# Decay factors by TensorE from sums of logarithms, and the float64 weights converted inside the attention

## The chip, the cores and the metric

The kernel runs on one core of one Trainium2 chip. The metric is the device time of one launch in microseconds (us). Five engines work side by side: TensorE (PE in the rows, with its weight loads as PEld), VectorE (DVE), ScalarE (ACT), GpSimd (POOL), and SyncE (SP), which here issues most DMAs. Each engine runs its own instructions in the order in which the program issued them; a semaphore holds an instruction, and all behind it on that engine, until what it needs is there.

## The reference

Three stages follow each other: a gated linear attention, an expert layer with a greedy routing of fixed capacity, and a feed-forward layer with ELU. The weights of the last stage, `w_in` and `w_out`, are float64.

```python
f = 1.0 / (1.0 + np.exp(-f_logit))                    # 4 batches, 8 heads, 768 steps, 48 channels
for t in range(S):
    state = f[:, :, t, :, None] * state + np.einsum('bhd,bhe->bhde', k[:, :, t], v[:, :, t])
    y[:, :, t] = np.einsum('bhd,bhde->bhe', q[:, :, t], state)
...
logits = x @ w_gate                                   # x: 3072 tokens of 384; 8 experts, 384 tokens each
for idx in np.argsort(-logits.flatten()):             # a token takes an expert that is not yet full
    ...
out[mask] = np.maximum(x[mask] @ w1[e], 0.0) @ w2[e]  # 384 -> 1024 -> 384, per expert
...
h = x @ w_in                                          # 384 -> 2048
return np.where(h > 0, h, np.exp(np.minimum(h, 0)) - 1) @ w_out
```

## The kernel before

**Attention** (lines 343 to 678). The 3072 tokens are 24 chunks of 128, six to a batch. Inside a chunk the recurrence is written with the running product W of 1/f: keys are multiplied by W, queries divided by it, and the chunk is then two small matrix products and a carried state. The layout has channels on partitions (two heads of 48 in slots of 64) and time along the row. The steps of a chunk, by name:

- `prepE` (line 420): ACT makes vv = 1 + exp(-f_logit) in two passes. `prepA` (line 428): DVE runs a scan over the 512 elements of a row, W, with a restart value `rst` at the head of each 128, and takes the last reciprocal into `pend`.
- `prepB`: ACT makes P = 1/W as exp(-ln W). `prepK`, `prepC` (lines 443 to 455): POOL makes kk = k W, aa = q P and W P; `prepD`: DVE makes qq = (2 - W P) aa, which takes out the error of the logarithm.
- `scores` (line 465): PE multiplies kk by qq, head by head; `masked`: DVE masks the result into `am`; `turn`: PE transposes kk, ACT copies it to `kn`.
- `ystep` (line 494): PE adds am v and S qq into y; PE makes kv, DVE puts it into the state SA (lines 518, 519), and `carry` copies the state on ACT to S, which the next chunk's matmul on line 507 reads.
- `xrows` (line 530): PE turns y to rows and multiplies it by `wg` (lp), ACT copies the rows, SP writes them to DRAM; `best` and `count` prepare the routing.

**Float64 words.** [...] The class `Conv` (line 258) takes a block of words as pairs of 32-bit integers and makes two float32r parts of them: `load` (a DMA into r64), `bits` (three DVE operations, lines 299, 303, 306, the middle one for the block before), `hi` (ACT, line 312) and `lo` (POOL, line 319). A block has 256 columns; there are 48. The tables ATT_CONV, SURE_CONV, GAP_CONV, F_CONV, M_AHEAD and M_CONV say how many are handled at which place: the 24 of `w_in` in the attention, the 24 of `w_out` after it, in the routing, in the first expert and in the first group.

**Routing and feed-forward.** After the attention a grid of thresholds finds the tokens whose expert is certain (lines 679 to 819; a branch for other inputs is not taken). Then PE works through eight experts, each with F1 (line 1056) and F2 (lines 1043 to 1045), and after each expert through a group of the last layer: A (line 1183, `w_in`) and B (`w_out`). Expert 0 goes first with 256 of its tokens, so that its 16 blocks of matmuls and its group cover the rest of the routing: rounds of `rows`, four `compare`s on DVE (lines 881 to 884), `ranks` on PE (line 891), `assign`, `left`, `again`, then `pick`. These stand between the matmuls at fixed places: a call of `tick` after each block of matmuls issues what is due. The experts' own weights are split into two parts by `feed` (ACT line 234, POOL line 227).

```python
blocks = wi_blocks + wo_blocks                     # line 251
r = self.pool.tile([128, 256, 2], I32, name="r64", bufs=4)
...
for _ in range(F_CONV[f]):                         # line 1141, in the first expert
    conv_stage()                                   # lo, hi, bits, load
```

Of the kernel before, what the change touches and what calls it, by code (L numbers as in the profile page):

```python
# [23 lines left out]
ATT_RAW = (11, 12)                          # chunks that load weights of the experts ahead  # L24
# [3 lines left out]
M_AHEAD = (0, 1, 1, 1)  # L28
M_CONV = (1, 2, 0, 2, 1, 2, 1, 0, 0, 2, 3, 3, 0, 0, 1, 2)
# [141 lines left out]
def kernel(ctx, tc, fT, kT, qT, v, wg, w12, win, w_out, out):  # L171
# [11 lines left out]
    win_h = wts.tile([128, 3 * 2048], F32R, name="win_h")  # L183
    win_l = wts.tile([128, 3 * 2048], F32R, name="win_l")
    WO1 = 6 * 384    # columns of w_out that are split early
    wout = [[wts.tile([128, WO1], F32R, name=f"wout{p}") for p in "hl"]]
# [3 lines left out]
    # the other experts run in the order in which they fill; None is the next of them  # L190
# [7 lines left out]
    # halves of the pieces, in the order of their use: w1 of f + 2, then w2 of f  # L198
# [8 lines left out]
    def raw():  # L207
        """Loads the next half, if its expert is known."""
# [12 lines left out]
    def feed(n, eng=None):  # L221
        """Splits up to n halves into their two parts; the low part of one goes with the high part of the next."""
# [15 lines left out]
    used = [-1, -1]     # the last piece whose w1, w2 were used before the current block  # L238
# [10 lines left out]
    wi_blocks = [("i", c, k) for k in range(8) for c in range(3)]  # L249
    wo_blocks = [("o", i) for i in range(24)]  # L250
    blocks = wi_blocks + wo_blocks

    def wo_cols(c, n):
        """Both parts of n columns of w_out."""
        k = c >= WO1
        return [t[:, c - k * WO1:c - k * WO1 + n] for t in wout[k]]
# [113 lines left out]
    load(0, "v")  # L370
    load(2, "f")
    load(1, "kq")
    load(2, "kq")
    load(1, "v")
    load(2, "v")
    for t in VT:
# [922 lines left out]
```

## Time and profile before

| what | us |
|---|---|
| three timed runs | 907.32, 914.92, 913.14 (median 913.14) |
| span of the profiled execution, first to last instruction | 910.4 |
| PE busy in it | 821.4 (90%) |
| DVE, ACT, POOL busy | 547.8, 443.5, 347.9 |
| mean granted TensorE clock, share of full speed | 0.935 |

The profile tells of one execution; its span is the only time that it gives of that one, and it lies 2.7 us under the median of the timed runs. An engine's busy time is the union of its instructions; waiting is not busy. The granted clock is given as a share: 1.00 is the upper level of 2.4 GHz, 0.5 the lower of 1.2 GHz, and a value between is a mean over time at both. In the attention DVE is busy nearly all the time, in the rest PE is.

### The profile page before, as it was taken

What the parts mean: (1) busy time and instruction counts of PE and PEld (TensorE: products, weight loads), DVE (VectorE), ACT (ScalarE), POOL (GpSimd) and SP (SyncE); (2) the same over time, 40 slices, a digit from 0 to 9 for tenths busy, and PEclk for the clock granted to TensorE, in tenths of its full rate; (3) what the DMA queues carried; (4) which work ended last, traced back from release to release, by engine and by line L of the source; (5) the groups of instructions that cost most, each with busy time, mean ns of one, the idle gap of its engine ahead of it and who ended that gap; (6) DMA issues with size and microseconds to landing.
All of it is one profiled execution on the core that took longest, in us unless ns stands there. A gap on an engine that the chain in (4) does not pass through costs nothing.

```text
span 910.4 us, 15321 instructions
## 1 busy us (share of the span) xinstructions
PE 821.4 (90%) x5573; PEld 776.8 (85%) x5573; DVE 547.8 (60%) x1245; ACT 443.5 (49%) x954; POOL 347.9 (38%) x379
## 2 busy tenths in 40 slices
PE   5977777895877799999999999999999999999996
PEld 4766666683867698999999999899999999999996
DVE  8799999987789867656756434533332432432332
ACT  5755555552344435444443544554444544544443
POOL 5667667844644654008103501351026107204101
PEclk7898897888777899999999999999999999999999
DMA  6556556433323332005101300630015004201000
GB/s 209 180 187 199 165 197 216 144 115 123 97 65 98 114 95 72 17 1 152 41 1 61 100 15 22 198 120 18 1 36 147 18 1 129 63 1 62 1 1 27
DMA packets 52037, 79.87 MB, mean 88 GB/s; under 512 B 9584, under 2 KB 34416, under 8 KB 51952
## 3 DMA queue, kind: packets, MB, share of 16 engines
q1 hardware_dynamic: 48752, 69.34, 24.6%
q0 software_dynamic: 3200, 9.46, 3.2%
q8 instruction: 46, 0.75, 0.3%
q14 instruction: 39, 0.32, 0.1%
HBM read 69.24 MB, written 9.54 MB: 87 GB/s over the span
## 4 chain that ended last, share of the span: by engine, by line
PE 54%; issue 9%; DVE 9%; POOL 2%; ACT 1%; POOLq 0%; DVEq 0%
PE ha L1183 18%; PE ha L1056 9%; PE yo L1043 9%; PE yo L1045 8%; PE yo L1044 8%; DVE oh L884 1%; DVE oh L881 1%; POOL pc_l L227 1%; PE ha L1038 1%; DVE w L306 1%; DVE w L299 1%; DVE w L303 1%; DVE oh L883 1%; DVE h_l L1061 1%; DVE elu L1187 0%
## 5 line engine op out<-in xcount | busy, mean ns | idle before, releaser
L227 POOL TENSOR_TENSOR pc_l<-raw,pc_h 128x384 fp32r<-128x384 f32 x128 | 131.4, 1049 | 84.6 <-ACT pc_h L234 57.2
L1187 DVE SCALAR_TENSOR_TENSOR elu<-elu,ha 128x384 f32<-128x384 f32 (+2 forms) x128 | 70.8, 553 | 151.6 <-ACT elu L1186 151.0
L1254 POOL DMA_INDIRECT out<-ot,permL x22 | 22.5, 1023 | 291.7 <-ACT ot L1252 288.4
L1183 PE MATMUL ha<-yt_h,win_h 128*128 128x384 f32 (+2 forms) x384 | 132.3, 345 | 0.5 <-DVE elu L1187 0.5
L1183 PE MATMUL ha<-yt_h,win_l 128*128 128x384 f32 (+2 forms) x384 | 130.9, 341 | 0.0
L1043 PE MATMUL yo<-wouth,g_h 128*128 128x384 f32 x381 | 130.5, 343 | 0.0
L1045 PE MATMUL yo<-wouth,g_l 128*128 128x384 f32 x381 | 129.5, 340 | 0.0
L1044 PE MATMUL yo<-woutl,g_h 128*128 128x384 f32 x381 | 129.0, 339 | 0.0
L1183 PE MATMUL ha<-yt_l,win_h 128*128 128x384 f32 (+2 forms) x384 | 127.0, 338 | 0.0
L1185 ACT ACTIVATE elu<-ha 128x384 f32<-128x384 f32 (+2 forms) x128 | 62.6, 489 | 114.6 <-PE ha L1183 114.5
L1025 ACT ACTIVATE g_h<-elu 128x384 fp32r<-128x384 f32 (+2 forms) x127 | 66.5, 523 | 75.9 <-DVE elu L1187 75.6
L1026 DVE TENSOR_TENSOR g_l<-elu,g_h 128x384 fp32r<-128x384 f32 (+2 forms) x112 | 66.1, 591 | 55.5 <-ACT g_h L1025 54.9
L1061 DVE SCALAR_TENSOR_TENSOR h_l<-ha,h_h 128x384 fp32r<-128x384 f32 (+2 forms) x72 | 36.8, 511 | 91.2 <-ACT h_h L1060 85.7
L1060 ACT ACTIVATE h_h<-ha 128x384 fp32r<-128x384 f32 (+2 forms) x72 | 32.6, 453 | 107.4 <-PE ha L1056 96.4
L1183 PEld LDWEIGHTS ha<-yt_h,win_h 128*128 128x128 f32 x384 | 73.9, 192 | 2.2 <-DVE elu L1187 0.7
L1183 PEld LDWEIGHTS ha<-yt_h,win_l 128*128 128x128 f32 x384 | 73.5, 191 | 2.2
L1183 PEld LDWEIGHTS ha<-yt_l,win_h 128*128 128x128 f32 x384 | 73.0, 191 | 1.4
L1043 PEld LDWEIGHTS yo<-wouth,g_h 128*128 128x128 f32 x381 | 72.4, 190 | 0.9 <-ACT g_h L1025 0.3
L1044 PEld LDWEIGHTS yo<-woutl,g_h 128*128 128x128 f32 x381 | 72.4, 190 | 0.6
L1056 PE MATMUL ha<-xt_h,pc_h 128*128 128x384 f32 (+2 forms) x216 | 71.3, 331 | 1.7 <-ACT pc_h L234 0.8
L1045 PEld LDWEIGHTS yo<-wouth,g_l 128*128 128x128 f32 x381 | 72.3, 190 | 0.3 <-DVE g_l L1026 0.3
L1056 PE MATMUL ha<-xt_h,pc_l 128*128 128x384 f32 (+2 forms) x216 | 71.2, 330 | 0.7 <-POOL pc_l L227 0.7
(248 smaller groups left out, 1831.5 us busy)
## 6 DMA issues: line engine op xcount, KB each, us to landing
raw<-w SPq DMA_DIRECT2D x144, 192.0 KB, 2.6
ld_k<-kT SPq DMA_DIRECT2D x24, 256.0 KB, 3.3
ld_q<-qT SPq DMA_DIRECT2D x24, 256.0 KB, 4.0
r<-win SPq DMA_DIRECT2D x24, 256.0 KB, 4.5
r<-wout SPq DMA_DIRECT2D x24, 256.0 KB, 2.7
ld_f<-fT SPq DMA_DIRECT2D x23, 256.0 KB, 4.1
vt<-v SPq DMA_DIRECT2D x24, 192.0 KB, 4.0
x_d<-x SPq DMA_DIRECT2D x24, 192.0 KB, 2.1
```

The costliest lines, as they stand in the source:

```text
L227: (eng or nc.gpsimd).tensor_tensor(l, RAW.pop(i), h.bitcast(F32), op=OP.subtract)
L1025: nc.scalar.activation(hi, src, AF.Copy)
L1026: (eng or nc.vector).tensor_tensor(lo, src, hi.bitcast(F32), op=OP.subtract)
L1043: nc.tensor.matmul(o, wh, mh, start=start, stop=False)
L1044: nc.tensor.matmul(o, wh, ml, start=False, stop=False)
L1045: nc.tensor.matmul(o, wl, mh, start=False, stop=stop)
L1056: nc.tensor.matmul(p[:, :n], a[:, d * 128:(d + 1) * 128], b[:, d, :n], start=i == 0, stop=i == 8)
L1060: nc.scalar.activation(h[:, :n], p[:, :n], AF.Relu)
L1061: nc.vector.scalar_tensor_tensor(l[:, :n], p[:, :n], 0.0, h[:, :n].bitcast(F32), op0=OP.max, op1=OP.subtract)
L1183: nc.tensor.matmul(p, a[:, d * 2048 + f * 128:d * 2048 + (f + 1) * 128], b[:, d, :N], start=i == 0, stop=i == 8)
L1185: nc.scalar.activation(e, p, AF.Relu, scale=-1.0)
L1187: nc.vector.scalar_tensor_tensor(e, e, -1.0, p, op0=OP.add, op1=OP.max)
```

## The change

The decay factors come from a sum of logarithms. `f_logit` is loaded a second way, token by token (`fN`); ACT makes u = ln(1 + exp(-f_logit)) in two passes (`decayE`, `decayL`), and PE multiplies u by the triangular mask, which sums it over time (`decays`, eight products into one PSUM tile L, channels on partitions). ACT makes W = exp(L), P = exp(-L) and `pend` from L. POOL makes kk, DVE qq = q P; the scan, the correction of P and two of POOL's three products are gone. The state is kept in the layout in which PE reads it, so ACT's copy of it is gone; the product with it has eight matmuls for four. The loop over the chunks issues each result one step ahead of its use. Scores have one buffer of two PSUM banks instead of three of one; W, P, u, x have fewer SBUF buffers.

The blocks of float64 words have 512 columns, there are 24, one per chunk, all of them in the attention; the tables for the later places are gone, and with them every conversion after the attention. `r64` has 2 buffers of 4 KB per partition instead of 4 of 2 KB. Both weights lie whole in SBUF from the start.

In the routing the comparison with the threshold uses a value `least` that ACT computes from tau, and a few checks of ranges are added.

```diff
-ATT_CONV = [0] * 4 + [2, 2, 1, 2, 1, 1, 2, 1, 1, 2, 1, 1, 2, 1, 1, 1, 2] + [0] * 3
-SURE_CONV, GAP_CONV, GAP_LOADS = 2, 5, 4
-F_CONV = (1, 1, 2, 1, 0, 1, 1, 0)
+ATT_CONV = range(0, 24)
-            r = self.pool.tile([128, 256, 2], I32, name="r64", bufs=4)
+            r = self.pool.tile([128, CW, 2], I32, name="r64", bufs=2)
-                w = self.pool.tile([128, 256], I32, name="w64", bufs=4)
+                w = self.pool.tile([128, CW], I32, name="w64", bufs=3)
-        nc.vector.tensor_tensor_scan(fl(W), fl(vv), fl(rst[:, h]), 1.0, op0=OP.mult, op1=OP.min)
+    L = ps.tile([112, 4, 128], F32, name="L")
...
+    def decayE(j):
+        if j < NJ:
+            nc.scalar.activation(buf(j, "u", [128, 384], 3), T[j]["f"], AF.Exp, scale=-1.0, accum_out=usum[:, j:j + 1])
+    def decayL(j):
+            nc.scalar.activation(u, u, AF.Ln, bias=1.0)
+    def decays(j):
+        for pr in range(4):
+            for s in range(2):
+                o = (2 * pr + s) * 48
+                nc.tensor.matmul(L[s * 64:s * 64 + 48, pr, :], u[:, o:o + 48], mask, start=True, stop=True)
+    def prepW(j):
+            nc.scalar.activation(buf(j, "W", HD, 1), L, AF.Exp)
+    def prepP(j):
+            nc.scalar.activation(buf(j, "P", HD, 1), L, AF.Exp, scale=-1.0)
+            nc.scalar.activation(pend[:, j], L[:, :, 127], AF.Exp, scale=-1.0)
...
-            SK[j] = [ps.tile([128, 4, 128], F32, name="sc", bufs=3) for s in range(2)]
+        SK[j] = ps.tile([128, 2, 4, 128], F32, name="sc")
...
-                nc.tensor.matmul(y[0:112, pr, :], Sc[:, pr].rearrange("p s e -> p (s e)")[:, :112],
-                                 c["qq"][0:112, pr], start=False, stop=True, skip_group_check=True)
+                for s in range(2):
+                    r = slice(s * 64, s * 64 + 48)
+                    nc.tensor.matmul(y[r, pr, :], S[j % 2][r, pr], C[j]["qq"][r, pr], start=False, stop=True,
+                                     skip_group_check=True)
...
-    for j in range(3, NJ):
+    for j in range(-5, NJ):
+            load(j + 7, "f")
+            load(j + 3, "kq")
+            load(j + 2, "v")
             conv.load()
+            prepW(j + 2); prepP(j + 2); prepK(j + 2)
+            state(j)
+            scores(j + 1); turn(j + 1)
+            xout(j - 2)
+            decayL(j + 4)
+        decayE(j + 5)
+            carry(j)
+            prepQ(j + 2)
+            lout(j - 2)
+        conv.lo()
+        conv.hi()
+        conv.bits()
+            turned(j + 1); masked(j + 1)
+            ystep(j); yout(j)
+            xrows(j - 1)
+            decays(j + 3)
...
-                    for _ in range(F_CONV[f]):
-                        conv_stage()
-            for _ in range(M_AHEAD[f] if si == NE else 0):
-                conv_stage()
```

The first place is VectorE in one chunk in the middle of the attention, of before, with one conversion block (w and r are the words of a block, SA the state, am the masked scores):

```order
L299 TENSOR_SCALAR w_1081<-r_1000 128x256
L303 SCALAR_TENSOR_TENSOR w_989<-r_901,w_989 128x256
L306 SCALAR_TENSOR_TENSOR w_1081<-r_1000,w_1081 128x256
L460 SCALAR_TENSOR_TENSOR qq<-P,aa 128x512
L491 TENSOR_TENSOR am_1124<-sc,mask 128x512
L491 TENSOR_TENSOR am_1125<-sc,mask 128x512
L432 TENSOR_SCALAR rst<-vv 128x4
L433 SCALAR_TENSOR_TENSOR W<-vv,rst 128x512
L434 RECIPROCAL pend<-W 128x4
L518 TENSOR_TENSOR SA<-kv,SA 112x192
L519 TENSOR_TENSOR SA<-SA,pend 112x192
L542 TENSOR_REDUCE Lall<-lp 128x8
```

The row of line 433 is the scan. The same engine in a chunk of the change:

```order
L497 TENSOR_TENSOR SA<-kv,S_149 112x192
L498 TENSOR_TENSOR S_148<-SA,pend 112x192
L445 TENSOR_TENSOR qq<-ld_q,P 112x512
L535 TENSOR_REDUCE Lall<-lp 128x8
L286 TENSOR_SCALAR w_1128<-r_1083 128x512
L290 SCALAR_TENSOR_TENSOR w_1033<-r_988,w_1033 128x512
L293 SCALAR_TENSOR_TENSOR w_1128<-r_1083,w_1128 128x512
L478 TENSOR_TENSOR am<-sc,mask 128x1024
```

The scan, its restart value and the reciprocal are gone, the conversion has blocks twice as wide, and the state stands at the head of the chunk, before the conversion. Line 286 reads the block r that this chunk loads, line 290 the block of the chunk before.

The second place is SyncE's queue of DMAs in one chunk of the attention, of before (ld_k, ld_q, ld_f, vt are the inputs, r the words of a block, x_d the rows of x):

```order
L363 DMA ld_k<-kT 128x512
L363 DMA ld_q<-qT 128x512
L360 DMA vt_105<-v 128x384
L363 DMA ld_f<-fT 128x512
L289 DMA r_1373<-win 128x512
L540 DMA x_d<-x 128x384
```

And of the change:

```order
L352 DMA ld_f<-fN 128x384
L355 DMA ld_k<-kT 112x512
L355 DMA ld_q<-qT 112x512
L349 DMA vt_103<-v 128x384
L276 DMA r_1175<-wout 128x1024
L532 DMA x_d<-x 128x384
```

The block of words has twice the bytes and still stands behind the four inputs; the inputs are a little smaller.

The third place is VectorE in the first round of the routing, inside expert 0, of before (oh and mr belong to the `compare`s, h_l to F1):

```order
L881 TENSOR_SCALAR oh<-mr,m_4414 128x128
L883 TENSOR_SCALAR oh<-mr,m_4414 128x384
L884 SCALAR_TENSOR_TENSOR oh<-mr,m_4414,triS 128x128
L299 TENSOR_SCALAR w_4702<-r_4560 128x256
L303 SCALAR_TENSOR_TENSOR w_4652<-r_4475,w_4652 128x256
L306 SCALAR_TENSOR_TENSOR w_4702<-r_4560,w_4702 128x256
L1061 SCALAR_TENSOR_TENSOR h_l<-ha,h_h 128x256
L881 TENSOR_SCALAR oh<-mr,m_4414 128x256
```

And of the change:

```order
L843 TENSOR_SCALAR oh<-mr,m_4396 128x128
L845 TENSOR_SCALAR oh<-mr,m_4396 128x384
L846 SCALAR_TENSOR_TENSOR oh<-mr,m_4396,triS 128x128
L1023 SCALAR_TENSOR_TENSOR h_l<-ha,h_h 128x256
L843 TENSOR_SCALAR oh<-mr,m_4396 128x256
```

The conversion between one comparison and the next is gone; the rest stands as it did.

## Rows read from the trace of the kernel before

**Rows 1.** Busy time of each engine in stretches of the span, with granted clock.

```profile
core 0: us, PE busy (x) PEld busy (x) DVE busy (x) ACT busy (x) POOL busy (x), PEclk, DMA share, GB/s
0.00:18.00 18.00, 9.02 (x61) 6.96 (x63) 15.39 (x33) 9.76 (x18) 9.38 (x23) 0.78 0.72 248
45.00:203.00 158.00, 126.81 (x1263) 107.14 (x1261) 152.53 (x313) 87.98 (x202) 107.25 (x83) 0.86 0.55 175
203.90:227.40 23.50, 12.84 (x130) 9.73 (x129) 16.54 (x48) 5.60 (x15) 9.60 (x23) 0.88 0.40 123
227.40:258.10 30.70, 25.51 (x172) 24.15 (x173) 25.09 (x63) 10.28 (x27) 18.25 (x21) 0.72 0.32 95
258.10:319.10 61.00, 44.65 (x313) 42.82 (x312) 52.14 (x140) 28.73 (x75) 34.02 (x43) 0.82 0.32 93
319.10:354.00 34.90, 32.44 (x201) 31.40 (x201) 25.26 (x51) 13.46 (x30) 18.06 (x19) 0.95 0.35 103
408.30:436.20 27.90, 26.81 (x193) 25.86 (x192) 19.81 (x43) 11.99 (x27) 19.76 (x22) 1.00 0.46 135
```

**Rows 2.** Timeline of TensorE at single places: start, duration, what (us).

```profile
3.55 4.12 PE L569 MATMUL sc<-triU,onesB 128*128 128x256 bf16 x22 [3.55 <-DVE onesB L386]
...
15.98 2.08 PE L503 MATMUL y<-am,vt 128*64 128x128 f32 x15 [3.36 <-DVE am L491]
...
199.71 1.10 PE L503 MATMUL y<-am,vt 128*64 128x128 f32 x16
200.73 1.13 PE L507 MATMUL y<-qq,S 112*112 112x128 f32 x8
201.70 1.05 PE L534 MATMUL lp<-IW,yt 112*128 112x120 f32 x8
```

**Rows 3.** Single lines of VectorE over the whole span: duration ns min/median/max.

```profile
L433 DVE TENSOR_TENSOR_SCAN W<-vv,rst x25: 692/1226/2334, 4.8 to 178.9; 128x512 f32<-128x512 f32 x23, 128x256 f32<-128x256 f32 x2
L306 DVE SCALAR_TENSOR_TENSOR w<-r,w x48: 409/418/1493, 55.7 to 302.2; 128x256 int32<-128x256 int32 x48
L299 DVE TENSOR_SCALAR w<-r x48: 278/289/1255, 55.4 to 301.6; 128x256 int32<-128x256 int32 x48
L460 DVE SCALAR_TENSOR_TENSOR qq<-P,aa x24: 426/680/1755, 8.6 to 192.7; 128x512 f32<-128x512 f32 x22, 128x256 f32<-128x256 f32 x2
L491 DVE TENSOR_TENSOR am<-sc,mask x56: 398/677/686, 15.5 to 198.5; 128x512 f32<-128x512 f32 x40, 128x256 f32<-128x256 f32 x16
L519 DVE TENSOR_TENSOR SA<-SA,pend x16: 357/766/1245, 28.6 to 199.5; 112x192 f32<-112x192 f32 x16
```

**Rows 4.** Groups of POOL in 45 to 203 us: busy us, mean ns.

```profile
L446 POOL TENSOR_TENSOR kk<-ld_k,W 128x512 f32<-128x512 f32 x17 | 23.9, 1409 | 18.7 <-DMA ld_k<-kT 10.4 <-DVE w L306 4.9 <-DVE qq L460 1.7
L319 POOL TENSOR_TENSOR win_l<-w,win_h 128x256 fp32r<-128x256 f32 x24 | 20.3, 851 | 5.5 <-ACT win_h L312 5.5
```

**Rows 5.** DMA issues in 30 to 200 us: size, median us from issue to landing.

```profile
r<-win SPq DMA_DIRECT2D x24, 256.0 KB, 4.5
```

**Rows 6.** What TensorE waited for in 227 to 350 us: total, times, longest.

```profile
PE rt L891 <- DVE oh L881: 14.6, 8, 3.9
PE rt L948 <- DVE oc L942: 4.1, 2, 3.5
```

**Rows 7.** Groups of VectorE and POOL in 227.4 to 319.1 us: busy us, mean ns.

```profile
L306 DVE SCALAR_TENSOR_TENSOR w<-r,w 128x256 int32<-128x256 int32 x20 | 12.0, 598 | 0.0
L303 DVE SCALAR_TENSOR_TENSOR w<-r,w 128x256 int32<-128x256 int32 x20 | 11.0, 552 | 0.0
L299 DVE TENSOR_SCALAR w<-r 128x256 int32<-128x256 int32 x20 | 8.1, 404 | 0.0
...
L319 POOL TENSOR_TENSOR woutl<-w,wouth 128x256 fp32r<-128x256 f32 x21 | 16.5, 791 | 3.4 <-ACT wouth L312 3.4
```

**Rows 8.** Timeline of TensorE inside expert 0: two matmuls that follow each other.

```profile
238.76 0.28 PE L1056 MATMUL ha<-xt_h,pc_h 128*128 128x256 f32 x1
238.88 0.28 PE L1056 MATMUL ha<-xt_l,pc_h 128*128 128x256 f32 x1
```

More of the change, by code (lines that the diff above doesn't have):

```diff
@@ L170, with kernel @@
 @with_exitstack
-def kernel(ctx, tc, fT, kT, qT, v, wg, w12, win, w_out, out):
+def kernel(ctx, tc, fN, fT, kT, qT, v, wg, w12, win, w_out, out):
     nc = tc.nc
@@ L247, in ready @@
         return PC.pop((g, k))
[L249 to L256, printed above, removed]
+    CW = 512
+    blocks = [b for k in range(4) for b in [("i", c, k) for c in range(3)] + [("o", 3 * k + c) for c in range(3)]]
     class Conv:
-        N = 48
-        CW = 256
+        N = 24
         def __init__(self):
@@ L341, with load @@
     tau = cst.tile([128, 1], F32, name="tau")
+    least = cst.tile([128, 1], BF, name="least")
     actx = ExitStack()
     att = actx.enter_context(tc.tile_pool(name="att", bufs=1))
-    ld = actx.enter_context(tc.tile_pool(name="ld", bufs=3))
-    wk = actx.enter_context(tc.tile_pool(name="wk", bufs=2))
+    ld = actx.enter_context(tc.tile_pool(name="ld", bufs=2))
+    wk = actx.enter_context(tc.tile_pool(name="wk", bufs=1))
     ps = actx.enter_context(tc.tile_pool(name="ps", bufs=1, space=PSUM))
     T = {}
-    VT = [att.tile([128, 400], F32, name=f"vt{i}") for i in range(4)]
-    def load(j, what="fkqv"):
+    VT = [att.tile([128, 400], F32, name=f"vt{i}") for i in range(3)]
+    def load(j, what):
         if j >= NJ:
@@ L463, with scores @@
     AM, KN, YT, SK = {}, {}, {}, {}
-    def scores(j, h=ALL):
+    def scores(j):
         if j >= NJ:
@@ new lines @@
+    spin(ps.tile([128, 1024], F32, name="sc"), WARM)
+    for j in range(-5, NJ):
+        real = 0 <= j
+        if j + 7 > 2:
+            load(j + 7, "f")
+        if j + 3 > 1:
+            load(j + 3, "kq")
+        if j + 2 > 1:
+            load(j + 2, "v")
+        if j in ATT_CONV:
+            conv.load()
+        if j + 2 >= 0:
+            prepW(j + 2)
+            prepP(j + 2)
+            prepK(j + 2)
+        if j >= 0:
+            state(j)
+        if j + 1 >= 0:
+            scores(j + 1)
+            turn(j + 1)
+        if j >= 2:
+            xout(j - 2)
+        if j + 4 >= 0:
+            decayL(j + 4)
+        decayE(j + 5)
+        if j >= 0:
+            carry(j)
+        if j + 2 >= 0:
+            prepQ(j + 2)
+        if j >= 2:
+            lout(j - 2)
+        conv.lo()
+        conv.hi()
+        conv.bits()
+        if j + 1 >= 0:
+            turned(j + 1)
+            masked(j + 1)
+        if j == 0:
+            grid_exp()
+        if j >= 4 and j % 3 == 1:
+            best(j - 4, j - 1)
+        if j >= 5 and j % 3 == 2:
+            count(j - 5, j - 2)
+        if j >= 0:
+            ystep(j)
+            yout(j)
@@ L798 @@
     f1 = md.tile([1, 1], F32, name="f1")
-    xg0 = [cst.tile([128, 384], F32, name=f"xg0{t}") for t in range(2)]
     def gather0():
@@ L811, in gatherL @@
                                          in_offset=bass.IndirectOffsetOnAxis(ap=permE[:, 24 + j:25 + j], axis=0))
-    slots(lambda: [conv.bits() for _ in range(SURE_CONV)])
+    slots()
     rv = nc.values_load(fi[0:1, 0:1], min_val=0, max_val=1, skip_runtime_bounds_check_because="a comparison gives 0 or 1")
@@ L1078, in F2 @@
             mm3(Y[si][d][:, :n], wh[:, w], wl[:, w], h[:, :n], l[:, :n], f == 0, f == 7)
-    def conv_stage():
-        conv.lo()
-        conv.hi()
-        conv.bits()
-        conv.load()
-    def conv_until(want):
-        n = max(blocks.index(b) for b in want) + 1
-        while conv.at["lo"] < n:
-            conv_stage()
-    spin(fp.tile([128, 512], F32, name="rt"), SPIN[3])
-    for k in range(GAP_CONV):
-        conv.lo()
-        if k < 3:
-            conv.hi()
-        conv.bits()
+    spin(fp.tile([128, 512], F32, name="rt"), SPIN[3])
     gatherL()
     xtrans(0)
-    for k in range(GAP_CONV - 3):
-        conv.hi()
-    for _ in range(GAP_LOADS):
-        conv.load()
     F1(0, 0)
@@ L1176, in A @@
         def A(f):
-            conv_until([("i", c, f // 2) for c in range(3)])
             p = fp.tile([128, 512], F32, name="ha", bufs=3)[:, :N]
@@ L1198, in B @@
         def B(f, ts=None):
-            conv_until([("o", i) for i in range(f * 384 // 256, ((f + 1) * 384 + 255) // 256)])
             h, l, e = G[f]
-            wh, wl = wo_cols(f * 384, 384)
+            wh, wl = (W["o" + p][:, f * 384:(f + 1) * 384] for p in "hl")
             for t in range(N // 128) if ts is None else ts:
@@ L1224 @@
             tick()
-            if si == NE and M_CONV[f]:
-                conv_stage()
             used[:] = [8 * si - 1, 8 * si - 1]
@@ L1242 @@
             tick()
-            for _ in range(M_CONV[f] - 1 if si == NE else 0):
-                conv_stage()
             if si == NE and f >= 14:
```

367 lines of the change are left out of this document (133 added, 234 removed).

## The prediction

> **What bounds the kernel now.** I read the stretches first. From 45 to 203 us, inside the attention, DVE is busy 152.53 of 158 us, PE 126.81 at a granted clock of 0.86, POOL 107.25, ACT 87.98 [rows 1]. So DVE sets the pace of a chunk there. The matmuls of line 503 start at 15.98 us for the first chunk and at 199.71 for the last [rows 2]: 183.7 us for 23 chunks, 7.99 each. Then the single lines of DVE: the scan takes 1226 ns at the median but up to 2334, the conversion's line 306 takes 418 and up to 1493, while the masks, which read PSUM, stay between 677 and 686 in the full shape [rows 3]. Operations with two SBUF operands are thus held up at times, and POOL is the other engine at work on SBUF, busy 5.4 us of each chunk.
>
> From 227.4 to 354 us (expert 0, its group, F1 and F2 of expert 1) PE should set the pace, and doesn't: it is busy 25.51 + 44.65 + 32.44 = 102.6 of 126.6 us, with a clock of 0.72, 0.82 and 0.95. In the same work of the next expert, 408.3 to 436.2, it is busy 26.81 of 27.9 at 1.00 [rows 1]. The list of waits names the cause: PE waits 14.6 us for the routing's comparisons on DVE and 4.1 for the operand of a pick [rows 6]. In 227.4 to 319.1 DVE spends 12.0 + 11.0 + 8.1 = 31.1 of its 77.2 busy us on conversion, and POOL 16.5 [rows 1, 7]; the conversions stand between the comparisons. After 354 us the diff changes nothing that PE waits for.
>
> **The change part by part: VectorE in a chunk.** Before, the named operations at their medians are scan 1.23, two masks 1.35, qq 0.68, and 24 blocks in 158 us, which is 1.2 blocks a chunk of 0.29 + 2 x 0.42, so 1.35: 4.6 of the 7.7 busy us (152.53 / 158 x 7.99). The other 3.1 are small operations and the holding up. After: qq 0.68, one mask of 1024 elements, 0.40 + 3 x 0.28 = 1.24 by the two shapes in the row, and one block of 512 columns, 0.57 + 2 x 0.70 = 1.97 if each 256 columns more cost 0.28 [rows 3]: 3.9. To it comes the 3.1, at most whole, and at least the state (0.36 for line 519 at its minimum, and one more like it) and small ones, 1.0. POOL keeps kk, 1.41, and the low part of a block, up to 2 x 0.85 [rows 4]: 3.1 instead of 5.4 per chunk, 4.1 in the last eight where experts' weights are split too, so the holding up shrinks with it. DVE per chunk: 4.9 to 7.0; I take 6.0.
>
> **TensorE in a chunk.** Busy 126.81 / 158 x 7.99 = 6.4 us. The sums of logarithms are eight products in the shape of line 503 (half the columns each), whose sixteen records take 200.73 - 199.71 = 1.02 us; the product with the state has eight for four, which is nothing if two run side by side on the array's halves, and at most the 0.97 from 200.73 to 201.70 once more [rows 2]; I take 0.2. That is 7.6 at a clock of 0.86, 6.5 at 1.00. ACT loses a copy of vv and the copies of the state and gains the wider block: it stays near its 87.98 / 158 x 7.99 = 4.4 and doesn't bound.
>
> **The block of words in a chunk.** The three `bits` operations of a chunk wait in order on DVE for this chunk's DMA, and r64 now has two buffers: the DMA of a block can be issued only when line 290 has read the block two before, one chunk earlier. Behind a late block DVE's mask is queued, and behind that PE's next `ystep`. This gives a loop of one chunk: issue, landing, line 286, line 290. A block of 256 KB lands 4.5 us after its issue [rows 5]; the second 256 KB at the 248 GB/s of the first 18 us [rows 1] are 1.06 more: 5.55. Issue takes some 0.4 (the front four of the queue are issued ahead of it), line 286 0.57, line 290 0.70: 7.2 us. From both sides: with 3.0 for the landing (two thirds of the row's 4.5) it is 4.7 and hidden under DVE and PE; with the five DMAs of a chunk, 1.38 MB, at the mean 175 GB/s of the attention [rows 1] and the block last, the landing is 7.9 and the loop 9.5. I take 7.2, the value nearest to the row, and since PE at 6.5 to 7.6 and DVE at 6.0 lie at or under it, a chunk of **7.2 us**: 23 x (7.99 - 7.2) = 18 less.
>
> The Trainium skill, DMA: Bandwidth & Descriptors, "Anatomy of one DMA", fits a fixed 2.0 us and the bytes at 436 GB/s. By it 256 KB would land in 2.6 us and 512 KB in 3.2; the row shows 4.5 for the first, so the queue in this kernel is not empty. By the page the loop would be an estimated 4.9 us and no bound, and the chunk that of the second case below.
>
> **Its ends.** PE is kept by the warm-up products until 3.55 + 4.12 = 7.67 us [rows 2], and the first sum, exp, two products, scores and mask follow one another after it: I put the first `ystep` 1 us later than 15.98 (between -1 and +3). At the end the last chunks wait for the last blocks, and DVE has six small checks more: +1.5 (0 to +3). In the routing stretch, 203.9 to 227.4 [rows 1], the conversions ahead of the ids and of expert 0's x go, and ACT's `least` comes in: -1 (-2 to +1).
>
> **Expert 0 to expert 1.** What is lost there against a PE that never waits at full clock is 126.6 - 102.6 = 24.0 us idle and 0.28 x 25.51 + 0.18 x 44.65 + 0.05 x 32.44 = 16.8 at the lower level of 1.2 GHz [rows 1]. The upper end of the gain is the stretch of the next expert: 4% idle, full clock, so 5 lost of 126.6 and 36 gained; the lower end is none, if the routing's own chain sets the pace. A round has four comparisons one `tick` apart, a tick is nine matmuls of 0.12 us [rows 8], 1.1 us, and DVE makes a comparison and a h_l in about that, so PE will still wait some, and POOL's split of the experts' weights still holds DVE up. I take two thirds of the 18.7 us of waits [rows 6], half of the other 5.3, and of the lower clock, which comes with waits, 10: 12.5 + 2.6 + 10 = **25 us less**. What hid the conversion before is PE's own work there; in the attention its new cover is the loop above.
>
> **The sum.** -18 + 1 + 1.5 - 1 - 25 = -41.5: the span goes from 910.4 to 868.9. The median of the runs lies 2.7 over the span, so the time is **871 us**. No change means 913; a measurement of this kernel can tell about 1% from none.
>
> **The rivals.**
> - *The block is hidden, and PE at full clock sets the chunk.* [...] Against it: the 4.5 us in rows 5. A chunk of 6.3: 23 x 1.7 = 39 instead of 18, so 850.
> - *The attention gains nothing*: twice the conversion per chunk, a product more on PE at 0.86 (7.6) and POOL's two operations fill the 8 us again. For it: DVE at 97% today. Against it: 1.2 us of scan and its holding up go. Chunk 7.9: 871 + 16 = 887.
> - *The routing's chain keeps the pace after the attention*: the comparisons are late by their own length and POOL's splits, not by the conversions. For it: in 319.1 to 354, with no conversion left, PE still loses 2.5 us idle and clock. Gain 10 for 25: 886.
> - *Slower: the two buffers of r64 starve DVE.* The block is issued last behind four inputs that all become free at once, and lands with the burst: 7.9 us at 175 GB/s, loop 9.5, 23 x 1.5 = 35 more instead of 18 less: 924. It decides from a chunk of 9.0 on. Against it: the mean rate is what the kernel asks for, not what the queues can do; the first 18 us show 248.
>
> **How the numbers follow.** Forecast 0.45; block hidden 0.22; attention without gain 0.16; routing chain 0.11; starved 0.06. The forecast's own range is 858 to 882. For 8 in 10 I go down past the second case with both terms good, 842, and up past the third and fourth with both poor, 898. Faster by over 1% (under 904): nearly all of the first four, 0.90; slower by over 1% (over 922): most of the last, 0.05; between: 0.05.
>
> **What would show it.** Right: chunks of about 7.2 us, DVE waiting at line 286 for the DMA of r in most chunks, landing near 5.5 us; no instruction of the conversion after 205 us; F1 of expert 1 some 20 us earlier against expert 0's start; waits of PE for comparisons down by two thirds. Wrong: chunks near 6.3 with a clock near 1.00 (second case); line 286 waiting for POOL or DVE without idle time at 8 (third); comparisons that still cost 14 us of waits (fourth); landings over 7 us (fifth). The prediction as a whole falls if the attention is longer than before, or if the stretch from expert 0 to the end of expert 1 doesn't shorten by at least 10 us.

## The result, and the profile after

The changed kernel takes 883.33 us (median of four runs: 878.09, 887.48, 889.45, 879.17), the kernel before 910.59 beside it: a ratio of 0.970, with a 95% interval of 0.964 to 0.976. The forecast was 871, with a range of 842 to 898. The profiled execution is the shortest of the four; its span is 876.4 us, 34.0 under the 910.4 of before.

| stretch of the span | before | after | difference | forecast |
|---|---|---|---|---|
| to the first `ystep` | 16.0 | 17.2 | +1.2 | +1 |
| first to last `ystep`, 23 chunks | 183.7 | 168.6 | -15.1 | -18 |
| last `ystep` to F1 of expert 0 | 27.7 | 30.5 | +2.8 | +0.5 |
| F1 of expert 0 to group A of expert 1 | 126.6 | 103.9 | -22.7 | -25 |
| from there to the end | 556.4 | 556.2 | -0.2 | 0 |

So a chunk takes 7.33 us (7.2 was forecast), and the rest came near its terms as well. Whether it came so for the reasons given is another matter. First the busy times in stretches of the kernel after, with columns as in [rows 1]: the attention, expert 0, its group, the start of expert 1, and the rest.

```profile
45.00:180.00 135.00, 116.62 (x1599) 99.34 (x1598) 116.78 (x188) 72.16 (x177) 57.75 (x44) 0.96 0.71 215
216.30:239.10 22.80, 20.98 (x173) 20.66 (x173) 16.26 (x42) 8.46 (x21) 10.32 (x11) 0.89 0.14 37
239.10:286.90 47.80, 40.92 (x313) 38.90 (x310) 33.36 (x102) 23.82 (x61) 20.49 (x27) 0.93 0.22 63
286.90:320.20 33.30, 30.82 (x201) 29.77 (x200) 24.00 (x50) 13.47 (x30) 18.40 (x19) 1.00 0.37 107
320.20:876.40 556.20, 546.01 (x3203) 533.31 (x3202) 238.97 (x558) 267.00 (x546) 135.91 (x157) 0.99 0.17 51
```

In the attention PE and DVE are now busy for the same share, 86% (116.62 and 116.78 of 135), which for a chunk of 7.33 us is 6.33 and 6.34; the clock is 0.96 instead of 0.86. In the three stretches behind the routing PE is idle 1.8 + 6.9 + 2.5 = 11.2 us instead of 24.0.

The timeline of PE at the products of line 507, for five of the 24 chunks, and at the end of the thresholds:

```profile
17.25 1.09 PE L507 MATMUL y<-am,vt 128*64 128x128 f32 x16
...
85.41 1.09 PE L507 MATMUL y<-am,vt 128*64 128x128 f32 x16
...
91.41 1.09 PE L507 MATMUL y<-am,vt 128*64 128x128 f32 x16
...
100.14 1.09 PE L507 MATMUL y<-am,vt 128*64 128x128 f32 x16
...
185.82 1.09 PE L507 MATMUL y<-am,vt 128*64 128x128 f32 x16
...
195.51 0.35 PE L651 MATMUL lp<-idn,nov 8*128 8x8 f32 x2 [0.60 <-DVE over L649]
```

The mean hides two kinds of chunk: from 85.41 to 91.41 one takes 6.00 us, the next 8.73. Over the steady part every third chunk (4, 7, ... 19, counted from 0) takes 8.5 at the mean and the ten between them 6.7, six of these 5.8 to 6.4. Line 651 starts 9.7 us behind the last chunk's products; its like in the kernel before started at 206.84, 7.1 behind. What every third chunk has more is `best`. The timeline of DVE and PE in the long chunk (the row of line 507 at 100.14 follows the last one):

```profile
95.31 1.21 DVE L478 TENSOR_TENSOR am<-sc,mask 128x1024 f32<-128x1024 f32 x1
...
96.45 0.16 DVE L541 TENSOR_REDUCE top<-Lall 128x3 f32<-128x24 f32 x1
...
97.29 0.96 DVE L547 TENSOR_TENSOR ohE<-bw,bm 128x24 bf16<-128x24 f32 x1
...
98.17 1.72 DVE L550 TENSOR_SCALAR ge<-grid,top 128x256 bf16<-128x256 bf16 x3
...
99.55 0.66 PE L555 MATMUL cnt<-ge,ohE 128*8 128x256 bf16 x3 [1.18 <-DVE ge L550]
99.81 0.68 DVE L445 TENSOR_TENSOR qq<-ld_q,P 112x512 f32<-112x512 f32 x1
```

From 96.45 to 99.81 DVE does nothing but `best`, 3.4 us, and PE, whose counting products stand ahead of line 507, waits for it. Half of these 3.4 us is holding up: GpSimd's two products (lines 441 and 306) run from 96.90 to 99.41 here. In chunk 19, with no product of GpSimd beside it, `best` takes 1.6 us, and the chunk 7.1. Next the waits in 45 to 180 us (what waited, for whom: us in total, times, longest), and the DMA issues of the words of 30 to 180 us:

```profile
PE sc L457 <- DVE am L478: 6.7, 5, 1.9
PE cnt L555 <- DVE ge L550: 6.5, 5, 1.6
...
DVE w L286 <- DMA r<-wout: 4.6, 3, 2.7
...
DVE w L286 <- DMA r<-win: 3.5, 5, 1.5
...
PE sc L457 <- DVE top L541: 2.4, 3, 1.3
```

```profile
r<-wout SPq DMA_DIRECT2D x11, 512.0 KB, 4.9
r<-win SPq DMA_DIRECT2D x10, 512.0 KB, 4.8
```

DVE waits for words in 8 of 18 chunks, 8.1 us together, 0.45 per chunk: not "in most". The first chunk loses most by it. There the block lands among the first inputs (the DMA engines are 95% busy from 18 to 24 us), line 286 waits, the mask stands behind it, and PE behind the mask:

```profile
23.23 0.43 DVE L286 TENSOR_SCALAR w<-r 128x512 int32<-128x512 int32 x1 [5.79 <-DMA r<-win]
24.30 1.22 DVE L478 TENSOR_TENSOR am<-sc,mask 128x1024 f32<-128x1024 f32 x1
...
25.66 2.08 PE L457 MATMUL sc<-qq,kk 48*128 48x128 f32 x16 [6.01 <-DVE am L478]
```

Last, the groups of DVE in 45 to 180 us, which answer to [rows 3], and PE's longest waits in 216.3 to 320.2, which answer to [rows 6]:

```profile
L445 DVE TENSOR_TENSOR qq<-ld_q,P 112x512 f32<-112x512 f32 x18 | 25.3, 1404 | 0.7 <-ACT P L436 0.4 <-DMA r<-win 0.4
L478 DVE TENSOR_TENSOR am<-sc,mask 128x1024 f32<-128x1024 f32 x19 | 23.1, 1214 | 0.0
L498 DVE TENSOR_TENSOR S<-SA,pend 112x192 f32<-112x192 f32 x13 | 14.0, 1079 | 0.4
...
L290 DVE SCALAR_TENSOR_TENSOR w<-r,w 128x512 int32<-128x512 int32 x18 | 12.3, 682 | 0.0
```

```profile
PE rt L853 <- DVE oh L843: 7.2, 6, 3.2
PE ha L1000 <- DVE h_l L1023: 1.9, 1, 1.9
PE rt L910 <- DVE oc L904: 1.2, 2, 0.6
```

### The profile page after: what moved, and what is told of

Same layout as the page of the kernel before. It is cut to its first block, busy times and chain, and to the rows that moved or that the text cites. A ratio compares the mean times of both kernels' runs of the same rounds, so it can differ in the third digit from the quotient of the medians.

```text
span 876.4 us, 16095 instructions
## 1 busy us (share of the span) xinstructions
PE 812.5 (93%) x6117; PEld 767.8 (88%) x6117; DVE 475.7 (54%) x1046; ACT 416.3 (48%) x911; POOL 267.9 (31%) x306
## 4 chain that ended last, share of the span: by engine, by line
PE 57%; issue 8%; DVE 6%; POOL 3%; ACT 1%; DMA 1%; POOLq 0%; another core or an unknown queue 0%; DVEq 0%; ACTq 0%
PE ha L1122 19%; PE ha L1018 9%; PE yo L1005 9%; PE yo L1007 9%; PE yo L1006 9%; DVE oh L846 1%; DVE oh L843 1%; POOL pc_l L222 1%; DVE oh L845 1%; PE ha L1000 1%; DMA xg<-x_d,permL 1%; POOL xg L982 1%; DVE h_l L1023 0%; DVE elu L1126 0%; POOL out L1186 0%
## 5 line engine op out<-in xcount | busy, mean ns | idle before, releaser
L1122 PE MATMUL ha<-yt_h,wi_h 128*128 128x384 f32 (+2 forms) x384 | 131.4, 342 | 0.3 <-DVE elu L1126 0.3
L1122 PE MATMUL ha<-yt_h,wi_l 128*128 128x384 f32 (+2 forms) x384 | 130.3, 339 | 0.0
L1005 PE MATMUL yo<-wo_h,g_h 128*128 128x384 f32 x381 | 130.1, 342 | 0.0
L1007 PE MATMUL yo<-wo_h,g_l 128*128 128x384 f32 x381 | 128.9, 338 | 0.0
L1006 PE MATMUL yo<-wo_l,g_h 128*128 128x384 f32 x381 | 128.7, 338 | 0.0
L1122 PE MATMUL ha<-yt_l,wi_h 128*128 128x384 f32 (+2 forms) x384 | 126.6, 337 | 0.0
L1122 PEld LDWEIGHTS ha<-yt_h,wi_h 128*128 128x128 f32 x384 | 72.8, 190 | 2.0 <-DVE elu L1126 0.5
L1122 PEld LDWEIGHTS ha<-yt_h,wi_l 128*128 128x128 f32 x384 | 72.5, 189 | 2.2
L1122 PEld LDWEIGHTS ha<-yt_l,wi_h 128*128 128x128 f32 x384 | 72.4, 189 | 1.4
L1006 PEld LDWEIGHTS yo<-wo_l,g_h 128*128 128x128 f32 x381 | 72.1, 189 | 0.6
```

The source lines that it names most:

```text
L1005: nc.tensor.matmul(o, wh, mh, start=start, stop=False)
L1006: nc.tensor.matmul(o, wh, ml, start=False, stop=False)
L1007: nc.tensor.matmul(o, wl, mh, start=False, stop=stop)
L1122: nc.tensor.matmul(p, a[:, d * 2048 + f * 128:d * 2048 + (f + 1) * 128], b[:, d, :N], start=i == 0, stop=i == 8)
```

## The experiments

They ask three things: what the conversions cost where they stood and where they stand, what sets the length of a chunk, and why a lighter VectorE alone doesn't make it shorter. "The attention" is always first to last `ystep`. A time without a range is that of one execution. In the diffs `...` marks cuts, and most conditions on the chunk number are left out.

**1. The conversions put back beside the first expert.** A second converter runs at the tables' old places:

```diff
+    for _ in range(4):                                      # after the attention
+        late_conv.load()
...
+                    for _ in range((1, 1, 2, 1, 0, 1, 1, 0)[f]):
+                        late_stage()                        # in the first expert
...
+            for _ in range((0, 1, 1, 1)[f] if si == NE else 0):
+                late_stage()
...
+            M = (1, 2, 0, 2, 1, 2, 1, 0, 0, 2, 3, 3, 0, 0, 1, 2)[f] if si == NE else 0
...
```

> The changed kernel with 24 further blocks of 248 columns loaded and converted at the places at which the kernel before converts w_out (4 loads and 2 blocks in the routing, 5 ahead of the first expert, the rest in it and in the first group); nobody reads them. From F1 of expert 0 to group A of expert 1 the kernel before took 126.6 us, the changed kernel 103.9. Theory A (what was gained there is the conversions alone, through the comparisons that VectorE makes late, and the lower clock behind the waits): 120 to 127. Theory B (it comes from the other edits of the change, such as the comparison with least and the weights that lie whole in SBUF): 102 to 108.

906.46 us. The three stretches behind the routing, and the longest of PE's waits in them:

```profile
222.70:252.10 29.40, 23.44 (x173) 22.09 (x173) 24.25 (x62) 10.44 (x27) 17.21 (x21) 0.85 0.34 98
252.10:312.40 60.30, 45.19 (x313) 42.96 (x311) 50.50 (x141) 28.58 (x75) 31.69 (x43) 0.85 0.31 92
312.40:345.90 33.50, 31.18 (x202) 30.20 (x202) 24.91 (x50) 13.46 (x30) 18.00 (x19) 1.00 0.36 107
```

```profile
PE rt L899 <- DVE oh L889: 14.6, 9, 4.8
```

They take 29.4 + 60.3 + 33.5 = 123.2 us, 19.3 more than 103.9, and the wait for the comparisons is back at the very 14.6 us of [rows 6]. Theory A holds: 19.3 of the 22.7 us gained there are the conversions, through DVE's late comparisons and the lower clock that goes with them (0.85 instead of 0.89 and 0.93). The other 3.4 stay with the other edits, with the blocks' 248 columns for 256, or with the spread of single executions. One thing more: the attention, whose code is that of the changed kernel, took 173.2 us here for 168.6.

**2. All words from one block.** In `load`, every block after the first takes the first one's r64:

```diff
+            if i == 0:
+                self.r = self.pool.tile([128, CW, 2], I32, name="r64", bufs=1)
...
-            self.t[i] = r
+            self.t[i] = self.r
```

> The changed kernel, but only the first block of float64 words is loaded, and all 24 blocks are converted from it (so the last layer's weights are not those of the reference); all operations of the conversion stay, the 23 other DMAs of 512 KB and the waiting for them go. Measured from the first product of line 507 to that of the last chunk: 168.6 us in the changed kernel (23 x 7.33). Theory A, the forecast (the loop of issue, landing, line 286 and line 290 through two buffers sets the pace of a chunk): chunks fall to TensorE's 6.3, so 145 us. Theory B (VectorE and TensorE are both full, and every third chunk is long because `best` is on VectorE in it): only the idle time before line 286 goes, 5.8 us in the first chunk and at most 0.45 in each other one, so 153 to 163, and every third chunk still takes over 8.

882.88 us, the attention 170.0: both expectations are missed as written, A by 25 us, B by 7. But the execution's TensorE was at the lower clock from 21.6 to 35 us and for some 20 us in all after 137. Chunks 4 to 15 ran at full clock here, and but for 3.4 us in the changed kernel too; the twelve took 80.1 us here and 85.3 there, 0.44 less per chunk. That is as much as line 286 waited, and a part of it can be those 3.4 us. Waiting for the DMA is worth no more, so it isn't what keeps chunks at 7.3. Of the four long ones among them two (4 and 10) stayed at 8.7, and two (7 and 13) fell to 6.6. The end of `best` in chunks 10 and 13:

```profile
95.45 0.95 DVE L546 TENSOR_TENSOR ohE<-bw,bm 128x24 bf16<-128x24 f32 x1
96.32 1.72 DVE L549 TENSOR_SCALAR ge<-grid,top 128x256 bf16<-128x256 bf16 x3
...
115.17 0.18 DVE L546 TENSOR_TENSOR ohE<-bw,bm 128x24 bf16<-128x24 f32 x1
115.27 0.67 DVE L549 TENSOR_SCALAR ge<-grid,top 128x256 bf16<-128x256 bf16 x3
```

Beside GpSimd's two products (95.06 to 97.56) `best` takes 3.4 us, ahead of them 1.6: in chunks 4 and 10 the one, in 7 and 13 the other. So the length of these chunks goes with what GpSimd does beside `best`; no run moved that alone.

**3. `best` and `count` after the loop.**

```diff
-        if j >= 4 and j % 3 == 1:
-            best(j - 4, j - 1)
-        if j >= 5 and j % 3 == 2:
-            count(j - 5, j - 2)
...
+    for j in range(0, NJ - 3, 3):
+        best(j, j + 3)
+        count(j, j + 3)
```

> The changed kernel with `best` and `count` of all chunks after the loop instead of every third chunk in it. Theory A (the loop through two buffers of words): the attention's 168.6 us stay within 3, since landing and buffers are the same, and the whole is some 20 longer by the seven groups that now stand at the end. Theory B (`best` in every third chunk, 3.3 us of VectorE, costs 2.2 us there): the long chunks of 8.2 to 8.7 go, all take 6.0 to 6.6, and the 168.6 become 148 to 155; the whole is about even, since the groups come back at the end.

883.74 us, the attention 155.3 (13.3 less), the tail to the end of the thresholds 14.4 longer.

```profile
45.00:170.00 125.00, 112.27 (x1600) 97.12 (x1596) 104.26 (x141) 72.16 (x177) 59.47 (x44) 0.97 0.74 234
```

With the same two buffers and the same DMAs of words, chunks 4 to 15 take 76.8 us, 6.4 each. So the loop through the two buffers can run at 6.4 or under; theory A, the forecast's, has fallen. `best` and `count` in every third chunk were 13 of the 168.6 us. With them the edit took away the DMA of the logits (line 551), behind which SyncE issued the words 0.8 to 1.6 us late in those chunks; number 2, with no words to wait for, still has 8.7 in two of them.

**4. No conversion in the attention, after and before.** Blocks other than the first are neither loaded nor taken apart by VectorE; ScalarE and GpSimd go on as they did. The edit in the kernel before is the same for its first 24 blocks:

```diff
+            if i > 0:
+                return                                   # in load
...
+            if k is not None and k > 0:
+                self.t[k] = self.w0                       # in bits
+                k = None
+            if i is not None and i > 0:
+                i = None
```

> The changed kernel with one block of float64 words loaded and converted; the other 23 DMAs and the three VectorE operations of each of those blocks are left out, ScalarE and GpSimd make the two parts of all 24 blocks from that one (so the weights of the last layer are not the reference's). It prices what the conversion costs the attention on VectorE and in DMA. VectorE loses 1.95 us of its 6.3 per chunk. Theory B (VectorE and TensorE both full, `best` on top): the chunks without `best` stay at TensorE's 6.0 to 6.3, those with it fall from 8.4 to 6.3 to 6.8, the attention's 168.6 us (first to last product of line 507) fall to 145 to 155; the gain by which the kernel would shrink is then nearly what the conversion costs where it now stands, against the 19 us that it cost beside the first expert. If the clock of TensorE after waits is what makes chunks long (theory C), the granted clock in the attention goes to 1.00 at the same time.

> The kernel before with the loads and VectorE operations of 23 of the 24 blocks of w_in left out in the attention (all parts are made from the first block, so the weights of the last layer are not the reference's). With the like run of the changed kernel (145.2 us from first to last y) it prices the decay by itself, free of any conversion. If VectorE is what bounds the kernel before (97% busy), its 183.7 us fall by 24 blocks of 1.13 to 1.35 us, to 150 to 158, and the new decay by itself gains only 5 to 13; if the operations of GpSimd and VectorE hold each other up and the chain through the scan sets the pace, they fall to 160 to 175, and the new decay gains 15 to 30.

After: 853.67 us, the attention 145.2, 6.31 a chunk. Before: 895.73, and 168.1. One row of each, of 45 to 160 and of 45 to 180 us:

```profile
45.00:160.00 115.00, 111.26 (x1623) 95.74 (x1624) 84.61 (x134) 71.55 (x177) 59.98 (x44) 1.00 0.55 168
```

```profile
45.00:180.00 135.00, 112.94 (x1161) 95.20 (x1162) 112.33 (x220) 83.95 (x194) 101.60 (x82) 0.86 0.49 155
```

This gives the balance of the attention. The new decay by itself, with no conversion on VectorE in either: 168.1 to 145.2, 22.9 us less. The conversion costs 183.7 - 168.1 = 15.6 in the kernel before (24 blocks of 256 columns) and 168.6 - 145.2 = 23.4 in the changed one (24 of 512): 7.8 more. 22.9 - 7.8 = 15.1, as measured. Each of the four times is that of one execution, and two executions of one attention differed by 4.6 us (number 1), so the 7.8 is rough. The second of the two expectations for the kernel before holds: without its conversion VectorE is busy 83% (112.33 of 135) and its chunks are still 7.3 us, with GpSimd busy 101.60 and the clock at 0.86. VectorE's load, at 97% in [rows 1], was thus not all that set its pace; which wait did was not tried apart. A part of the 22.9 us is the clock, 1.00 in the one and 0.86 in the other.

**5. The mask ahead of qq.** Line 445 takes 1404 ns at the mean, 677 at the least: in 45 to 180 us the five that ran beside no product of GpSimd took 677 to 684, and of the thirteen beside one eight took 1756 to 1767. The mask, which reads PSUM, took 1207 to 1225 either way. The Trainium skill, GPSIMD Engine Reference, "Specifications", says that VectorE's instructions with two SBUF inputs contend with GpSimd for its SBUF interfaces; by it the mask could stand there at no price, and the trace agrees: its 1214 ns are the same beside GpSimd.

```diff
+            masked(j + 1)
             prepQ(j + 2)
             lout(j - 2)
...
-            masked(j + 1)
```

> The changed kernel with line 478 (the mask, which reads PSUM) issued on VectorE ahead of line 445 (qq, two SBUF operands) in each chunk, so that the mask and not qq stands beside GpSimd's two products. Theory A: a chunk stays at 7.3 (168.6 us in all), since the wait for words is only moved. Theory B: line 445 falls from a mean of 1404 ns to about 700, VectorE has 0.7 us less per chunk, and what it doesn't hide behind TensorE goes: the long chunks fall by 0.7 to 1, the others by up to 0.2, so 157 to 163, and the whole is 6 to 12 us faster than the changed kernel.

882.06 us (879.63 to 884.83), the attention 170.8: missed. Line 445 did fall, to 842 ns, and VectorE to 107.95 of 138 us. But a wait came up that the changed kernel has only for 1.9 us, PE's line 527 for the tile that lout frees, behind the mask and qq:

```profile
PE lp L527 <- DVE Lall L535: 11.6, 11, 3.6
```

**6. lout first.**

```diff
+            lout(j - 2)
             carry(j)
             masked(j + 1)
             prepQ(j + 2)
-            lout(j - 2)
```

> Line 535 (lout) first, then the state, the mask, qq and the conversion, in each chunk on VectorE: the mask still stands beside GpSimd's products, but the product of line 527 need not wait for line 535 behind the mask, as it did for 11.6 us in the last try. Theory B: this wait goes to under 2 us, line 445 stays near 840 ns, the attention takes 155 to 163 us (170.8 in the last try, 168.6 in the changed kernel); the chunks with `best` stay over 7.2. Theory C (the clock falls whenever TensorE waits some 1.5 us and that costs more than the waits themselves): fewer waits in the third chunks, a clock of 0.97 or more.

879.30 us, the attention 170.7: missed again. PE's wait for line 535 is gone, and line 445 is at its full speed, but now VectorE waits itself. Line 535 reads the tile that ScalarE copies in line 531, and now waits for that copy:

```profile
DVE Lall L535 <- ACT x L531: 25.5, 10, 5.6
PE cnt L555 <- DVE ge L550: 16.3, 6, 4.2
```

Theory C's "whenever" doesn't hold either: behind a wait of 2.09 us at 74.96 PE's products of line 507 still took 1.09 us, full clock.

Two further kernels keep this order. The first spreads the comparisons and counts them a chunk later, the second also takes line 290 into the chunk of lines 286 and 293:

```diff
+            best(j - 4, j - 1, False)                     # every third chunk, without line 550
...
+            j0 = (j - 4) // 3 * 3
+            ge(j0 + (j - 4) % 3)                          # every chunk: line 550 for one chunk of tokens
...
+            count(j - 5, j - 4)
```

```diff
-ATT_CONV = range(0, 24)
+ATT_CONV = range(-1, 23)
...
-            k = self.take("frac", "bits")
             i = self.take("bits", "load")
+            k = self.take("frac", "bits")
```

> As the one before, and the comparisons with the grid (line 550, three in one chunk) spread over three chunks, each counted on TensorE one chunk later. Theory B: no chunk has more than 6.8 us of VectorE, the third chunks fall from 8 to 6.3 to 7.0 and the attention to 147 to 155 us. If the length of the third chunks comes from something else than VectorE's load, they stay over 7.5.

> As the one before, and line 290 in the same chunk as lines 286 and 293 (each block leaves its buffer a chunk earlier), with every block loaded one chunk ahead. Theory B and the forecast's loop together: no wait of line 286 for DMA in the steady part, the first chunk 4 to 6 us instead of 11.4, chunks of 6.1 to 6.5: 142 to 150 us for the attention, the tail after it 1 to 2.5 us shorter, and 850 to 862 us in all against 883 for the changed kernel.

875.44 us with an attention of 162.7, and 878.86 (873.49 to 885.07) with 165.8. Both missed: line 535 still waited 25.6 and 17.7 us for line 531, and the third chunks stayed at 8.4 and 8.6. In the second one the bits moved ahead together with the loads, so that the first chunk remained at 10.9. No wait for words over 0.8 us was left in its steady part, and it gained nothing by that.

**7. State, mask, lout, qq: and the clock.**

```diff
             carry(j)
+            masked(j + 1)
+            lout(j - 2)
             prepQ(j + 2)
-            lout(j - 2)
...
-            masked(j + 1)
```

> The changed kernel with VectorE's order in a chunk state, mask, lout (line 535), qq, conversion. Against the two earlier orders: lout stands neither behind qq (TensorE's line 527 waited 11.6 us for it) nor ahead of the state (where it waited 25.5 us itself for ScalarE's copy of line 531). Theory B: both waits under 4 us between 45 and 180 us, line 445 at 680 to 850 ns instead of 1404, the attention (first to last product of line 507) 157 to 164 us against 168.6 and 170 to 173 in two other executions of the same code. Theory C (a wait of TensorE brings the lower clock, and that is worth more than the wait): chunks with a wait over 1.5 us are followed by one of 9 to 10 us.

878.50 us (874.49 to 886.03). Line 535 waits no more, line 527 for 0.9 us in all, VectorE has 108.56 of 140 us, 5.8 per chunk instead of 6.34, and still the attention takes 171.4. The row of 45 to 185 us, and the timeline of PE at one of the long chunks:

```profile
45.00:185.00 140.00, 126.56 (x1606) 107.90 (x1606) 108.56 (x190) 71.80 (x178) 59.93 (x44) 0.89 0.67 206
```

```profile
74.16 0.66 PE L555 MATMUL cnt<-ge,ohE 128*8 128x256 bf16 x3 [2.35 <-DVE ge L550]
74.75 1.09 PE L507 MATMUL y<-am,vt 128*64 128x128 f32 x16
75.77 1.95 PE L513 MATMUL y<-qq,S 48*48 48x128 f32 x16
77.65 2.04 PE L527 MATMUL lp<-IW,yt 112*128 112x104 f32 x8
```

PE waits 2.35 us for the comparisons, and from 75.77 on the same sixteen products take 1.95 us that took 1.08 before, the eight of line 527 2.04 instead of 1.1: the lower of the two levels, 1.2 GHz. Of its triples of chunks, the two at full clock (4 to 6 and 10 to 12) take 8.0 + 6.2 + 5.2 = 19.4 us; chunks 10 to 12 took 21.3 in the changed kernel. The triple with this wait (7 to 9) takes 9.4 + 9.3 + 5.6 = 24.3, for 20.5 there. Numbers 5 and 6 had lost clock too: 0.91, 0.90, 0.93 and 0.93 in their steady part, for 0.96. So there was a gain, and the clock seems to have taken it back. If so, products that nobody reads, put into that wait, should give it:

```diff
         if j >= 5 and j % 3 == 2:
+            YT[j] = ps.tile([128, 4, 128], F32, name="y")
+            spin(YT[j].rearrange("p r t -> p (r t)"), 14)
             count(j - 5, j - 2)
```

> The last order but one (state, mask, lout, qq, conversion) with 14 products of 128x256 that nobody reads (0.12 us each at full clock) on TensorE ahead of the counting products, the place at which it waited 12.0 us for line 550 in every third chunk. Theory C (the gain of that order is given back because the lower clock follows the waits): the granted clock between 45 and 185 us rises from 0.89 to 0.95 or more, the chunks of 9.3 to 10.3 us go, and the attention falls from 171.4 to 152 to 160 us although TensorE has 11 us of products more. If the clock has nothing to do with these waits, the attention grows by up to 11 us and its clock stays under 0.92.

866.09 us (864.37 to 868.94), a ratio of 0.952 to the kernel before (0.949 to 0.955); the attention 156.3, the clock 1.00:

```profile
45.00:170.00 125.00, 119.11 (x1648) 101.80 (x1648) 107.61 (x187) 69.34 (x171) 56.51 (x42) 1.00 0.73 226
```

Theory C holds here: one edit, which only adds work, takes 12 us from the whole by the medians. The 15 us that it takes from the attention are an upper figure, since the profiled execution of the kernel without it was the longest of its five (886.03). Its four runs lie within 4.6 us of each other, the five without it within 11.5.

**8. The waits taken away instead.** The order of number 7, one comparison with the grid a chunk, the counting products at the end of PE's chunk, line 290 in the chunk of lines 286 and 293, and each block loaded one chunk ahead:

```diff
-            k = self.take("frac", "bits")
             i = self.take("bits", "load")
+            k = self.take("frac", "bits")
...
-        conv.lo()
-        conv.hi()
-        conv.bits()
+        if j >= 0:                                        # no bits ahead of the first chunk
+            conv.lo()
+            conv.hi()
+            conv.bits()
...
+        if j >= 4:
+            ge(j - 4)
...
             decays(j + 3)
+        if j >= 5:
+            count(j - 5, j - 4)
```

> As the one before, and: line 290 in the same chunk as lines 286 and 293, each block loaded one chunk before its bits are taken, one comparison with the grid a chunk, and the counting products at the end of TensorE's chunk instead of ahead of line 507. Theory B: no wait for DMA at line 286, TensorE waits under 0.7 us per chunk, the first chunk 4 to 6 us, the third ones under 7.2: 146 to 155 us for the attention, and 855 to 868 us in all.

863.11 us (856.20 to 864.74), a ratio of 0.944 to the kernel before (0.939 to 0.949) and the shortest of those that do the whole work; the attention is 146.6, the first chunk 4.2, the third ones 6.2. Its tail is 3.4 us longer than the changed kernel's. No wait of line 286 for words is left, and of PE's only one kind over the whole of 45 to 165 us:

```profile
45.00:165.00 120.00, 115.14 (x1554) 95.99 (x1553) 101.08 (x187) 69.54 (x171) 53.22 (x43) 0.96 0.76 233
```

```profile
PE lp L524 <- DVE Lall L532: 4.9, 4, 2.0
```

PE is busy 96% of the time. Its longest wait, 2.0 us at 124.9, was again followed by 10.2 us at the lower clock and a chunk of 12.2.

## Why the prediction was right, and where it was not

- **The sum.** -34.0 us of span for -41.5: 2.9 are missing from the chunks, 0.2 from the start, 2.3 from the tail and the routing, 2.3 from the experts, and 0.2 came at the end. Of the rest of the 12.3 us between 871 and 883.33, 0.6 is rounding (868.9 + 2.7 is 871.6) and 4.2 the step "the median of the runs lies 2.7 over the span": it lies 6.9 over this one. The two long runs have a mean clock of 0.962 and spans of 885.8 and 887.7, the profiled one 0.973 and 876.4, and number 1 shows the same attention taking 4.6 us more. The size of the clock's share in one execution was not in the sum at all.
- **VectorE, PE, GpSimd and ScalarE in a chunk**: VectorE 6.0 forecast and 6.34 measured; PE 6.5 to 7.6 at a clock of 1.00 to 0.86 forecast and 6.33 at 0.96 measured; GpSimd 3.1 and 3.1 (57.75 of 135); ScalarE 4.4 and 3.9. The new operations came out as extrapolated: the mask 1.24 and 1.21, the block 1.97 and 1.79 by medians (0.43, 0.68, 0.68).
- **The step that failed: "This gives a loop of one chunk ... 7.2 us".** The landing takes 4.8 to 4.9 at the median, not 5.55, and in 10 of 18 chunks its issue follows line 290 at once (line 290 ends at 102.98, the block's DMA starts at 103.01), without the 0.4; with lines 286 and 290 the loop is 4.85 + 0.43 + 0.68 = 6.0. It hides under the 5.8 to 6.4 us of most chunks without `best` (number 3: 6.4 with this loop). By its mechanism the first rival, "the block is hidden", was nearer. What neither had is `best`: its 3.4 us, 1.8 of them held up beside GpSimd, were counted as "small ones" and holding up in a mean over three chunks, where they stand whole in one, on an engine with no time left. 7.33 beside 7.2 is luck: a number agrees, its reason doesn't. By the Trainium skill, DMA: Bandwidth & Descriptors, "Anatomy of one DMA", whose fit is of DMAs that GpSimd issues, 512 KB would land in an estimated 3.2 us; the trace's 4.8 differ. The DMAs here are SyncE's, so the prediction's 4.5 us beside the page's figure doesn't show a queue that is not empty; that the loop is no bound came true.
- **The start**: +1 and +1.2. But the first chunk's 11.4 us, of which 5.8 wait for its block, were not forecast; number 8 has it at 4.2.
- **The tail and the routing**: the tail took 2.6 more (1.5 forecast, up to 3), since a block's three operations, `best` and the checks stand on VectorE ahead of the last logits; the routing 0.3 more instead of 1 less.
- **Expert 0 to expert 1**: right in kind, shown by number 1. Idle time fell by 12.8 us (15.1 forecast), PE's busy time, the clock's part, by 102.6 - 92.7 = 9.9 (10 forecast). The waits for comparisons fell to 7.2, by half and not by two thirds: those comparisons are late by themselves, as the fourth rival said of all of them.
- **The other rivals.** "The attention gains nothing" had the cover right, not the size: the wider conversion gave back 7.8 of 22.9 us. "r64 starves DVE" fell with the landings, 8.1 us of waits in 18 chunks.

## What to carry to other kernels

When a step runs every third round, look at the round that holds it, not at the mean: the longest rounds set the time once an engine has no slack. Before a wait is made shorter, see what TensorE's clock does behind it; products that fill a wait can shorten the whole, although they only add work (number 7). And when an operation moves within an engine's order, look at the tiles that it frees and the copies that it shares: numbers 5 and 6 each traded one wait for another. See also what GpSimd does at that time: the same `best` took 1.6 or 3.4 us.

## What the runs showed of the hardware

- TensorE's clock fell to the lower level behind single waits (2.35 us at 74.16, number 7; 2.0 at 124.9, number 8), and 14 products that nobody reads, in every third chunk, raised the mean of the attention from 0.89 to 1.00. Not every such wait had this effect: behind 2.09 us at 74.96 and 2.90 us at 138.51 (both in number 6) the next products of line 507 took 1.09 us, full clock.
- VectorE's qq needed 677 ns alone and about 1757 beside a GpSimd product, an operation from PSUM the same 1214 either way. `best` took 1.6 us alone and 3.4 to 3.8 where it stood beside two such products.
